# A 2-D Fourier transform and a gated feed-forward layer on one core: second weight chunk folded in halves around the second stage, weight bits of two chunks made later, fewer and larger spills

## The chip, the cores and the metric

The kernel runs on one core of a Trainium2 chip. The metric is the device time of one launch in microseconds (us); lower is better. The times shown are medians of several executions. One more execution was recorded by the hardware profiler, and every duration below comes from that recording. Engines are named as the profile names them: PE is the matmul engine and PEld its weight loads, DVE, ACT and POOL are the three elementwise engines, and SP issues the DMAs.

## The reference

x is (8, 3008, 256), w_in (256, 2048), w_out (2048, 256), all float32; the output is (24064, 256).

```python
X = np.fft.fft(x, axis=1)          # over the sequence, 3008 = 47 * 64
X = np.fft.fft(X, axis=2).real     # over the width, 256
h = X.reshape(24064, 256) @ w_in
g = h * (1.0 / (1.0 + np.exp(-1.702 * h)))
out = g @ w_out
```

## The kernel before

**The pieces of the computation.** The transform over the width is not done on the data. It is multiplied into the first weight matrix instead: `fold_w(n)` multiplies a cosine and a sine matrix by 512 columns of w_in (chunk n of four) and leaves the result in two tiles `wcs[0]` and `wcs[1]`; ACT copies it there out of two PSUM banks called `psw`. The transform over the sequence has two stages. The first one (`mix_first` for batch 0; `fold1` on POOL with `mix1` on PE for batches 1 to 7) leaves its result in the tile `xt`, or `made` for batch 0. `spill` writes it to device memory `Td`, `fill` reads it back in another order as the tile t4, `rotate` multiplies one column, and `stage2` does the second stage on PE; DVE transposes its result out of PSUM (L361) into `pq`.

**The steps.** Each of the 8 batches has 3 blocks of 512 rows, each block two halves of up to 256 rows, and each half goes through 8 steps, one for each pair of 128-column pieces of the 2048 hidden columns: 384 steps, 48 to a batch. A step is a first matmul (pq times wcs), the activation, and a second matmul (`product`) with `wo`, the second weight matrix. Steps 0 to 7, while the weights are still being made, use a plain form: `hidden(t)` (two PSUM banks pa and pb, L183; ACT copies pa to v, L519), `rows(t)` on DVE (L557, L560, L548: sums of pa, pb and the row nb that `nyquist` made), `activate(t)` on ACT, `product(t)`, issued three steps later. From step 8 on, both matmuls have a form with fewer multiplications and more sums on DVE and POOL (`begin`, `forward`, `backward`, `sums`, `small_products`). Chunk n of w_in serves steps 2n and 2n+1 of each half, and chunk n of w_out likewise.

**Weights.** Both matrices are converted chunk by chunk from 64-bit words of which the kernel uses the two 32-bit halves. For one chunk: `load_in`/`load_out` (a DMA of 1 MB into one of three `raw` slots), `squares` (ACT L405), `clamp` (POOL L410), `low_up` and `low_down` (ACT L415, L420), `high` (three DVE operations, L437 to L439, called the masks below; the last leaves the masked word in the ring "a"), and the adding of the low bits, `finish_in` (POOL L451, into the tile `wst`) or `finish_out` (two POOL operations L459, into `wo`). `bounds` is squares, clamp, low_up and low_down together. The call takes the chunk's key: in0 to in3 and out0 to out3. The tile `big` holds these buffers as rings: "s" (squares), "m" (clamped words), "r" (low bits), "a", "raw", "h" (the activations of the plain steps).

**What sets the order.** There is no scheduler: every engine carries out its own instructions in the order of the program text, and semaphores hold an instruction until its operands are there. The opening is written out by hand up to `finish_out(0)`. Then one loop runs over the steps; `at(t, fn)` puts a call at the end of step t, `early` puts `fold_w(2)` and `fold_w(3)` inside steps 3 and 5, and `rows_at` puts `first_row(n)` (small matmuls `psf` from row 0 of wcs[1], copied to af1 and af2 by ACT) inside steps 1, 4 and 6. All DMAs of the main loop stand in one queue on SP, also in the order of the text, and each waits for the landing of the one eight places before it. `paced(t)` is a DMA of one word out of the data that step t makes; as SP issues in order, it holds back the DMAs after it until then.

**Banks.** `spare` is a list of six PSUM banks, b0 b1 b2 o2 o3 o4. Each call of `bank` takes the first and puts it at the end, so who meets whom in a bank depends on the number of calls before. `hidden(5)` names its banks b0 and b1 outright. `warm(1)` is one matmul of 128x512 whose result nobody reads; it takes a bank too.

**Later batches.** In batch b (starting at step t0 = 48 b; `late` is 5 for batch 0 and 0 for the others), the next batch's first stage runs in steps t0+6 to t0+21 on POOL; each of the four `mix1` is followed a step later by two spills of 192 KB; `fill` is issued in three parts from t0+27, `rotate` at t0+36, and `stage2` of the next batch at t0+40. The x of the batch after that is loaded from t0+31.

Of the kernel before, what the change touches and what calls it, by code (L numbers as in the profile page):

```python
# [46 lines left out]
def view(ap, offset, *dims):  # L47
    return bass.AP(ap.tensor, ap.offset + offset, [list(d) for d in dims])
# [63 lines left out]
def kernel(ctx: ExitStack, tc, x, w_in, w_out, tab1, tab2, out):  # L112
# [17 lines left out]

    Xr = [nc.dram_tensor(f"Xr{b}", (NA, NJ, D), F32, kind="Internal").ap() for b in range(B)]
    Nd = nc.dram_tensor("Nd", (B * NBLK, 512), F32, kind="Internal").ap()
    Tk = nc.dram_tensor("Tk", (B * NBLK * NF, 1), F32, kind="Internal").ap()
    Td = [nc.dram_tensor(f"Td{b}", (NG * 128, D), F32, kind="Internal").ap() for b in range(B)]

    w1 = const.tile([128, (NJ + 3) * NM + 64 - NM], F32, tag="w1", name="w1")
# [13 lines left out]
    o_banks = [psp.tile([128, 512], F32, tag=f"o{i}", name=f"o{i}") for i in range(2)]  # L150
    rest = psu.enter_context(tc.tile_pool(name="psu", bufs=1, space=PS))
    big = cv.tile([128, 19 * 1024], F32, tag="big", name="big")
    rings = {"s": (0, 1024, 3), "a": (3072, 1024, 1), "raw": (4096, 2048, 3), "h": (10240, 1024, 4), "r": (14336, 1024, 2),
             "m": (16384, 1024, 2)}
    turns = {}

# [11 lines left out]
    def bank(name, tag=None):  # L168
        if tag is None:
            tag = spare.pop(0)  # L170
            spare.append(tag)
        if tag in ("o0", "o1"):
            return o_banks[int(tag[1])]
        return (rest if tag[0] == "o" else psp).tile([128, 512], F32, tag=tag, name=name)
# [149 lines left out]
        for _ in range(n):  # L324
            nc.tensor.matmul(ps[:], lhsT=wcs[0][:, 0:128], rhs=wcs[0][:, 0:512], start=True, stop=True)

    def spill(b, c, q):

        nc.sync.dma_start(out=view(Td[b], (16 * c + 4 * q) * D, [NJ * D, NM], [1, 4 * D]),
                          in_=xt[64 * c:64 * c + NM, 4 * q:4 * q + 4, :].rearrange("p q d -> p (q d)"))  # L330

    def fill(b, a0=0, a1=NG):
        if a0 == 0:
# [42 lines left out]
    def nyquist_out(b, blk):  # L376
        i = b * NBLK + blk
        nc.sync.dma_start(out=Nd[i:i + 1, :], in_=pqt[b, blk][0:1, 1, :])

    def paced(t):  # L380
        nc.sync.dma_start(out=Tk[t:t + 1, :], in_=big[0:1, at_left(t, A11):at_left(t, A11) + 1])

    raw = {}

# [83 lines left out]
        for out, i0, i1 in ((t1, b12, b11), (t2, b22, t1), (t3, b22, b12), (t4, b21, t2)):  # L468
            nc.gpsimd.tensor_tensor(out, i0, i1, op=ALU.subtract)

    def fold_w(n):
        ps = [bank("psw") for _ in range(2)]
        for i in range(2):
            for cs in range(2):
                halves(ps[cs][:], cd[:, i, cs, :], wst[n][:, i, :], start=(i == 0), stop=(i == 1))
        for cs in range(2):

            nc.scalar.copy(wcs[cs][:, n * 512:(n + 1) * 512].rearrange("p (f c) -> p f c", f=4),
                           free(ps[cs][:], 0, [1, 4], [4, 128]))
# [42 lines left out]
    def at_left(t, q):  # L522
        return LEFT + t % 4 * 1024 + q * 256
# [356 lines left out]
        spill_first(k, 16, NM, (nc.sync, nc.sync))  # L880
    prepare(in1)
    squares(in1, nc.scalar)
    for h0 in (0, 512):
        finish_in(0, h0, 512)
    clamp(in1)
    low_up(in1)
    low_down(in1)
    high(in1)
    load_out(1, nc.sync)
    fill(0, 4, NG)  # L890
    warm(1)
    fold_w(0)
    warm(1)
    first_row(0)
    prepare(out0)
    finish_in(1)
    clamp(out0)
    rotate(0, 0, 4, nc.scalar.copy)
    squares(out0, nc.scalar)
    stage2(0, 0)  # L900
    warm(1)
    low_up(out0)
    low_down(out0)
    high(out0)
    load_in(3, nc.sync)
    prepare(in2)
    squares(in2, nc.scalar)
    clamp(in2)
    fold_w(1)
    finish_out(0)  # L910

    extra, early = {}, {}

    def at(t, fn, *args):
        extra.setdefault(t, []).append((fn, args))

    n = len(steps)

    for t, key in (1, in2), (2, ("out", 1)), (3, ("in", 3)), (5, ("out", 2)), (6, ("out", 3)):
        at(t, high, key)  # L920
        if key != in2:
            at(t - 1, bounds, key)
        at(t + 1, finish, key)
    early[3], early[5] = 2, 3
    rows_at = {1: 1, 4: 2, 6: 3}
    for t, c in ((0, 2), (1, 3)):
        at(t, load_out, c, nc.sync)
    at(3, load_matrices)
    if B > 1:
# [8 lines left out]
    for b in range(B):  # L938
        t0 = b * NBLK * NF
        late = 0 if b else 5  # L940
        if b + 2 < B:
            for k in range(3):
                at(t0 + 11 + k, paced, t0 + 11 + k)
                at(t0 + 11 + k, turn, b + 2, k)
        if b + 1 < B:
            for c in range(NCH):
                for part in range(2):
                    at(t0 + 6 + 2 * c + part + late, fold1, b + 1, c, part, nc.gpsimd)
                if c % 2:
                    k = t0 + 9 + 2 * c + late + (late > 0 and c == 5)  # L950
                    at(k, mix1, b + 1, c // 2)
                    for half in range(2):
                        at(k + 1, spill, b + 1, half, c // 2)
            for blk in range(NBLK):
                at(t0 + 27 + blk + late, paced, t0 + 27 + blk + late)
                at(t0 + 27 + blk + late, fill, b + 1, 4 * blk, 4 * blk + 4)
            if b + 2 < B:
                for k in range(4):
                    at(t0 + 31 + 2 * k + late, paced, t0 + 31 + 2 * k + late)
                    at(t0 + 31 + 2 * k + late, load_x, b + 2, k)  # L960
            at(t0 + 36 + 3 * (late > 0), rotate, b + 1)
        for blk in range(NBLK):
            nxt = (b, blk + 1) if blk + 1 < NBLK else (b + 1, 0)
            if nxt[0] < B:
                at(t0 + blk * NF + 8, stage2, *nxt)
                at(t0 + blk * NF + 9, nyquist_out, *nxt)
                at(t0 + blk * NF + 10, nyquist, *nxt)

    for t in range(n + LAG):
        if t < NP:  # L970
            if t == NP - 3:
                spare[:] = [tag for tag in spare if tag[0] == "o"] + ["b2"]
            hidden(t)
            if t == NP - 1:
                middle(NP)
                begin(NP)
                for c0 in range(0, DF, 1024):
                    nc.sync.dma_start(out=wcs[1][0:1, c0:c0 + 1024], in_=tab1[127:128, n0 + 4:n0 + 1028])
            if t == 0:
                low_up(in2)  # L980
                nyquist(0, 0)
                low_down(in2)
            if t in rows_at:
                first_row(rows_at[t])
            if t >= LAG:
                product(t - LAG, 0, None)
            if t in early:
                fold_w(early[t])
            if t:
                activate(t - 1)  # L990
            rows(t)
            if t == NP - 1:
                doubled(NP)
                middle(NP + 1)
        else:
            after, special = (any(fn in (mix1, stage2) for fn, _ in extra.get(k, ())) for k in (t - 1, t))
            if t < n:
                begin(t, 1)
            if t == NP:
                activate(t - 1)  # L1000
            if t < n:
                forward(t)
            if after and t + 1 < n:
                middle(t + 1)
            opening = (t - LAG) % NP == 0 and t >= NP + LAG
            one, other = (t - LAG, (1, 2, 4, 7)), (t - LAG - 1, (5, 6, 3))
            if opening:
                small_products(*other)
            cut = 0 if opening and not after else 3 if after else 2
            product(t - LAG, 0, cut)  # L1010
            if after:
                small_products(one[0], one[1][:1])
                small_products(other[0], () if opening else other[1][:1])
            if t + 1 < n:
                begin(t + 1)
            if not opening:
                small_products(other[0], other[1][after:])
            product(t - LAG, cut, 6 if t - LAG == last else None)
            small_products(one[0], one[1][after:])
            swap(t - LAG - 2)  # L1020
            if t < n:
                backward(t)
            if t + 1 < n:
                doubled(t + 1)
            if t < n:
                activate_back(t)
                sums(t, nc.gpsimd)
            if t + 2 < n and not special:
                middle(t + 2)
            combine_small(t - LAG - 1)  # L1030
            if t - LAG == last:
                product(last, 6, None)
            sums(t - 1, nc.vector)
            deeper(t - 2, 0)
            deeper(t - 3, 1)
        if t == NP:
            psu.close()
            low = ctx.enter_context(tc.tile_pool(name="low", bufs=1, space=PS))
            pot["low"] = low.tile([128, 3 * 512], F32, tag="low", name="low")
        if t >= LAG:  # L1040
            combine(t - LAG)
            combine_last(t - LAG - 2)
            turn_last(t - LAG - 3, 0)
            turn_last(t - LAG - 4, 1)
        if t >= NP:
            spare[:] = [f"b{t % 2}"] * special + ["b2"]
        for fn, args in extra.get(t, ()):
            fn(*args)
# [28 lines left out]
```

## Time and profile before

| | us |
|---|---|
| median of 3 runs (1861.98 to 1864.17) | 1862.27 |
| the profiled execution's own time | 1861.98 |
| its span on the core | 1860.2 |
| mean granted PE clock, share of full | 0.999 |
| PE busy | 1843.6 (99% of the span) |
| DVE / ACT / POOL busy | 1522.8 / 1150.2 / 963.2 |
| first matmul of step 0, `hidden(0)` | 39.85 |
| first matmul of step 5, `hidden(5)` | 63.20 |
| start of step 48 to start of step 96 (batch 1 to batch 2) | 276.11 to 501.58 |

The opening, in which the weights are converted and the first batch is transformed, lies in the first 86 us; step 8, the first of the second form, follows it. From there the batches repeat every 225.1 to 225.5 us. In a row of a stretch by engines the columns are the stretch, its length, the busy time and count of instructions of PE, PEld, DVE, ACT, POOL and SP, the granted clock, the busy share of the DMA engines, and what they moved in GB/s. A row of a timeline gives the start, the duration, the engine, the line, the operation, out <- in, the shapes, how many instructions went together, and in square brackets the idle time before it and who ended it. A row of the waits names the waiting group, the one that released it, the idle us in sum, how many, and the longest.

### The profile page before, as it was taken

What the parts mean: (1) busy time and instruction counts of PE and PEld (TensorE: products, weight loads), DVE (VectorE), ACT (ScalarE), POOL (GpSimd) and SP (SyncE); (2) the same over time, 40 slices, a digit from 0 to 9 for tenths busy, and PEclk for the clock granted to TensorE, in tenths of its full rate; (3) what the DMA queues carried; (4) which work ended last, traced back from release to release, by engine and by line L of the source; (5) the groups of instructions that cost most, each with busy time, mean ns of one, the idle gap of its engine ahead of it and who ended that gap; (6) DMA issues with size and microseconds to landing.
All of it is one profiled execution on the core that took longest, in us unless ns stands there. A gap on an engine that the chain in (4) does not pass through costs nothing.

```text
span 1860.2 us, 56005 instructions
## 1 busy us (share of the span) xinstructions
PE 1843.6 (99%) x23684; PEld 1404.9 (76%) x23684; DVE 1522.8 (82%) x2229; ACT 1150.2 (62%) x2248; POOL 963.2 (52%) x1057
## 2 busy tenths in 40 slices
PE   8999999999999999999999999999999999999998
PEld 5677777777777777777777777777777777778776
DVE  7888788888798877987789878888888888878874
ACT  6656666666656656666665666656666666656663
POOL 4676446744367444773347643476445754434442
PEclk9999999999999999999999999999999999999999
DMA  8721340215012240213302132031411111100111
GB/s 269 190 61 34 80 72 19 71 49 102 19 35 56 67 84 18 60 37 87 63 13 65 44 86 52 17 76 34 102 30 25 36 46 35 31 19 13 22 20 24
DMA packets 148507, 105.31 MB, mean 57 GB/s; under 512 B 105961, under 2 KB 129033, under 8 KB 147744
## 3 DMA queue, kind: packets, MB, share of 16 engines
q1 hardware_dynamic: 147040, 101.20, 23.7%
q8 instruction: 187, 3.06, 0.7%
q10 hardware_dynamic: 1216, 0.52, 0.1%
q14 instruction: 64, 0.52, 0.1%
HBM read 64.41 MB, written 48.05 MB: 60 GB/s over the span
## 4 chain that ended last, share of the span: by engine, by line
PE 87%; DVE 6%; ACT 3%; POOL 1%; DMA 1%; issue 1%; SPq 0%; DVEq 0%; ACTq 0%; POOLq 0%
PE x L183 32%; PE o L183 24%; PE low L668 23%; PE o L668 4%; DVE big L634 2%; PE ps L355 1%; PE ps L254 1%; DVE big L769 1%; DVE big L548 1%; ACT x L575 1%; DMA big<-in_moe_w_in_dram 1%; ACT big L590 0%; DVE big L612 0%; DMA wo<-in_tab_dram 0%; ACT g L587 0%
## 5 line engine op out<-in xcount | busy, mean ns | idle before, releaser
L605 POOL TENSOR_TENSOR big<-big 128x256 f32<-128x256 f32 (+1 forms) x376 | 349.9, 931 | 840.0 <-ACT big L597 732.2
L183 PE MATMUL x<-pq,wcs 128*64 128x256 f32 (+1 forms) x6016 | 771.3, 377 | 3.5 <-ACT g L587 2.2
L634 DVE TENSOR_TENSOR big<-big 128x512 f32<-128x512 f32 (+1 forms) x736 | 636.2, 879 | 30.6 <-PE low L668 14.2
L183 PE MATMUL o<-big,wo 128*64 128x256 f32 (+1 forms) x4800 | 621.1, 375 | 0.0
L183 PEld LDWEIGHTS x<-pq,wcs 128*64 128x64 f32 x6016 | 410.0, 137 | 193.7 <-issue 15.0
L183 PEld LDWEIGHTS o<-big,wo 128*64 128x64 f32 x4800 | 341.8, 137 | 146.7 <-DVE big L612 0.5
L587 ACT ACTIVATE g<-x 128x512 f32<-128x512 f32 (+1 forms) x376 | 222.0, 590 | 372.8 <-PE x L183 371.7
L548 DVE TENSOR_TENSOR big<-g,x 128x512 f32<-128x512 f32 (+2 forms) x440 | 253.8, 588 | 200.2 <-ACT big L590 199.8
L668 PE MATMUL low<-big 128*64 128x128 f32 (+1 forms) x5888 | 381.8, 270 | 0.0
L575 ACT ACTIVATE x<-nb,af 128x256 f32<-128x256 f32 (+1 forms) x752 | 352.7, 469 | 12.2
L606 POOL TENSOR_TENSOR big<-big 128x256 f32<-128x256 f32 (+1 forms) x376 | 358.7, 954 | 0.0
L668 PEld LDWEIGHTS low<-big 128*64 128x64 f32 x5888 | 337.0, 137 | 28.7
L590 ACT ACTIVATE big<-x 128x512 f32<-128x512 f32 (+1 forms) x376 | 220.5, 587 | 195.4 <-PE x L183 161.5
L597 ACT ACTIVATE big<-big 128x512 f32<-128x512 f32 (+1 forms) x376 | 231.8, 617 | 42.3 <-DVE big L548 40.4
L668 PE MATMUL low<-big,wo 128*64 128x128 f32 (+1 forms) x2944 | 220.2, 270 | 0.1
L668 PEld LDWEIGHTS low<-big,wo 128*64 128x64 f32 x2944 | 171.9, 137 | 3.8 <-DVE big L634 0.4
L613 DVE TENSOR_TENSOR big<-big 128x512 f32<-128x512 f32 (+1 forms) x188 | 147.7, 786 | 6.5
L612 DVE TENSOR_TENSOR big<-big 128x512 f32<-128x512 f32 (+1 forms) x188 | 136.9, 728 | 5.4 <-POOL big L605 5.4
L769 DVE TENSOR_TENSOR big<-big,low 128x512 f32<-128x512 f32 (+3 forms) x184 | 109.1, 610 | 3.5
L668 PEld LDWEIGHTS o<-big,wo 128*64 128x64 f32 x1472 | 92.2, 137 | 25.0
L668 PE MATMUL o<-big,wo 128*64 128x128 f32 (+1 forms) x1472 | 110.0, 270 | 0.0
L226 POOL TENSOR_TENSOR xt<-xt 111x510 f32<-111x510 f32 x56 | 77.2, 1379 | 4.4
(102 smaller groups left out, 965.0 us busy)
## 6 DMA issues: line engine op xcount, KB each, us to landing
out_dram<-os SPq DMA_DIRECT2D x284, 64.0 KB
t<-Td SPq DMA_DIRECT2D x22, 512.0 KB
Td<-xt SPq DMA_DIRECT2D x56, 192.0 KB
xt<-in_x_dram SPq DMA_DIRECT2D x14, 512.0 KB
xt<-Xr SPq DMA_DIRECT2D x14, 512.0 KB
nb<-Nd SPq DMA_DIRECT2D x23, 256.0 KB
out_dram<-os SPq DMA_DIRECT2D x96, 56.0 KB
Xr<-in_x_dram SPq DMA_DIRECT2D x7, 752.0 KB
```

Of the source, the lines that this page charges most:

```text
L183: nc.tensor.matmul(out[c0:c0 + 64], lhsT=lhs[:, c0:c0 + 64], rhs=rhs, skip_group_check=True, **how)
L548: nc.vector.tensor_tensor(free(out, at + m - 1, [by, 2], [RUN, blocks], [-1, m]), *ins, op=op)
L575: nc.scalar.activation(x[:, i * 256:i * 256 + n], nbt[b, blk][:, hh * 256:hh * 256 + n], ACTF.Copy, scale=af1[:, f:f + 1])
L587: nc.scalar.activation(two(g[:], n), two(xb[t][:], n), ACTF.Copy, scale=2.0)
L590: nc.scalar.activation(front(t), two(xb[t][:], width(t)), ACTF.Gelu_apprx_sigmoid)
L597: nc.scalar.activation(back(t), back(t), ACTF.Gelu_apprx_sigmoid)
L605: eng.tensor_tensor(right(t, S1, n), left(t, A21, n), right(t, A22, n), op=ALU.add)
L606: eng.tensor_tensor(left(t, S3, n), left(t, A11, n), left(t, A21, n), op=ALU.subtract)
L612: eng.tensor_tensor(s2, s1, a11, op=ALU.subtract)
L613: eng.tensor_tensor(s4, a12, s2, op=ALU.subtract)
L634: nc.vector.tensor_tensor(out, i0, i1, op=how)
L668: nc.tensor.matmul(o, lhsT=lhs, rhs=rhs, start=first_in, stop=(p == NP - 2), skip_group_check=True)
```

## The change

Seven things change together.

1. The tokens (`paced`, 63 one-word DMAs) are gone.
2. The first stage's result is spilled in two DMAs of 768 KB per batch, at steps t0+24 and t0+25 (+ late), in place of eight of 192 KB. `fill` and the load of the next x are issued one step later than before.
3. In the opening, `fold_w(1)` is split: its first half, over the first 128 rows of the chunk, stands before `rotate` and `stage2(0, 0)`, its second half after them; `high(in1)` and `finish_in(1)` are done in halves for it, and `clamp(in1)` stands between the two halves of `finish_in(0)`.
4. Two of the three `warm(1)` are gone.
5. `first_row(0)` stands after `fold_w(1)`; `finish_out(0)` moves to the end of step 1; `low_up(out0)` and `low_down(out0)` move into steps 0 and 1.
6. squares, low_up and low_down of in2 move into step 1, `bounds(out1)` from the end of step 1 to the end of step 2; the loads of out2 and out3 go from the ends of steps 0 and 1 to those of steps 1 and 2, and `load_in(3)` into step 0.
7. Ring "s" has two slots in place of three, ring "a" two in place of one.

```diff
-    rings = {"s": (0, 1024, 3), "a": (3072, 1024, 1), "raw": ...
+    rings = {"s": (0, 1024, 2), "a": (2048, 1024, 2), "raw": ...
...
-    def spill(b, c, q):
-        nc.sync.dma_start(out=view(Td[b], (16 * c + 4 * q) * D, [NJ * D, NM], [1, 4 * D]),
-                          in_=xt[64 * c:64 * c + NM, 4 * q:4 * q + 4, :].rearrange("p q d -> p (q d)"))
+    def spill(b, c):
+        nc.sync.dma_start(out=view(Td[b], 16 * c * D, [NJ * D, NM], [1, 16 * D]),
+                          in_=xt[64 * c:64 * c + NM, 0:16, :].rearrange("p q d -> p (q d)"))
...
-    def paced(t):
-        nc.sync.dma_start(out=Tk[t:t + 1, :], in_=big[0:1, at_left(t, A11):at_left(t, A11) + 1])
...
-    def fold_w(n):
-        ps = [bank("psw") for _ in range(2)]
-        for i in range(2):
+    folded = {}
+    def fold_w(n, parts=(0, 1)):
+        if parts[0] == 0:
+            folded[n] = [bank("psw") for _ in range(2)]
+        ps = folded[n]
+        for i in parts:
             for cs in range(2):
                 halves(ps[cs][:], cd[:, i, cs, :], wst[n][:, i, :], start=(i == 0), stop=(i == 1))
+        if parts[-1] == 0:
+            return
...
-    for h0 in (0, 512):
-        finish_in(0, h0, 512)
+    finish_in(0, 0, 512)
     clamp(in1)
+    finish_in(0, 512, 512)
     low_up(in1)
     low_down(in1)
-    high(in1)
+    for h0 in (0, 512):
+        high(in1, h0, 512)
     load_out(1, nc.sync)
     fill(0, 4, NG)
     warm(1)
     fold_w(0)
-    warm(1)
+    prepare(out0)
+    for h0 in (0, 512):
+        finish_in(1, h0, 512)
+    clamp(out0)
+    fold_w(1, (0,))
+    rotate(0, 0, 4, nc.scalar.copy)
+    stage2(0, 0)
+    squares(out0, nc.scalar)
+    fold_w(1, (1,))
     first_row(0)
-    prepare(out0)
-    finish_in(1)
-    clamp(out0)
-    rotate(0, 0, 4, nc.scalar.copy)
-    squares(out0, nc.scalar)
-    stage2(0, 0)
-    warm(1)
-    low_up(out0)
-    low_down(out0)
     high(out0)
-    load_in(3, nc.sync)
     prepare(in2)
-    squares(in2, nc.scalar)
     clamp(in2)
-    fold_w(1)
-    finish_out(0)
...
-    for t, key in (1, in2), (2, ("out", 1)), (3, ("in", 3)), (5, ("out", 2)), (6, ("out", 3)):
+    at(1, finish_out, 0)
+    at(1, high, in2)
+    at(1, finish, in2)
+    at(2, bounds, ("out", 1))
+    for t, key in (2, ("out", 1)), (3, ("in", 3)), (5, ("out", 2)), (6, ("out", 3)):
         at(t, high, key)
-        if key != in2:
+        if t > 2:
             at(t - 1, bounds, key)
         at(t + 1, finish, key)
...
-    for t, c in ((0, 2), (1, 3)):
+    for t, c in ((1, 2), (2, 3)):
         at(t, load_out, c, nc.sync)
...
-                    for half in range(2):
-                        at(k + 1, spill, b + 1, half, c // 2)
+            for c in range(2):
+                at(t0 + 24 + c + late, spill, b + 1, c)
             for blk in range(NBLK):
-                at(t0 + 27 + blk + late, paced, t0 + 27 + blk + late)
-                at(t0 + 27 + blk + late, fill, b + 1, 4 * blk, 4 * blk + 4)
+                at(t0 + 28 + blk + late, fill, b + 1, 4 * blk, 4 * blk + 4)
...
             if t == 0:
-                low_up(in2)
                 nyquist(0, 0)
-                low_down(in2)
+                low_up(out0)
+                load_in(3, nc.sync)
+            if t == 1:
+                low_down(out0)
             if t in rows_at:
                 first_row(rows_at[t])
+            if t == 1:
+                squares(in2, nc.scalar)
+                low_up(in2)
+                low_down(in2)
```

Here `finish(in2)` stands at the end of step 1, right after `high(in2)`; before, it stood at the end of step 2, behind `bounds(out1)`, which stood at the end of step 1.

More of the change, by code (lines that the diff above doesn't have):

```diff
@@ L132 @@
     Nd = nc.dram_tensor("Nd", (B * NBLK, 512), F32, kind="Internal").ap()
-    Tk = nc.dram_tensor("Tk", (B * NBLK * NF, 1), F32, kind="Internal").ap()
     Td = [nc.dram_tensor(f"Td{b}", (NG * 128, D), F32, kind="Internal").ap() for b in range(B)]
@@ L152 @@
     big = cv.tile([128, 19 * 1024], F32, tag="big", name="big")
-    rings = {"s": (0, 1024, 3), "a": (3072, 1024, 1), "raw": (4096, 2048, 3), "h": (10240, 1024, 4), "r": (14336, 1024, 2),
+    rings = {"s": (0, 1024, 2), "a": (2048, 1024, 2), "raw": (4096, 2048, 3), "h": (10240, 1024, 4), "r": (14336, 1024, 2),
              "m": (16384, 1024, 2)}
@@ L942 @@
             for k in range(3):
-                at(t0 + 11 + k, paced, t0 + 11 + k)
                 at(t0 + 11 + k, turn, b + 2, k)
@@ L949 @@
                 if c % 2:
-                    k = t0 + 9 + 2 * c + late + (late > 0 and c == 5)
-                    at(k, mix1, b + 1, c // 2)
-                    for half in range(2):
-                        at(k + 1, spill, b + 1, half, c // 2)
+                    at(t0 + 9 + 2 * c + late + (late > 0 and c == 5), mix1, b + 1, c // 2)
+            for c in range(2):
+                at(t0 + 24 + c + late, spill, b + 1, c)
             for blk in range(NBLK):
-                at(t0 + 27 + blk + late, paced, t0 + 27 + blk + late)
-                at(t0 + 27 + blk + late, fill, b + 1, 4 * blk, 4 * blk + 4)
+                at(t0 + 28 + blk + late, fill, b + 1, 4 * blk, 4 * blk + 4)
             if b + 2 < B:
                 for k in range(4):
-                    at(t0 + 31 + 2 * k + late, paced, t0 + 31 + 2 * k + late)
-                    at(t0 + 31 + 2 * k + late, load_x, b + 2, k)
+                    at(t0 + 32 + 2 * k + late, load_x, b + 2, k)
             at(t0 + 36 + 3 * (late > 0), rotate, b + 1)
```

## The prediction

> **What bounds the kernel now.** I read the page's busy table first, then the busy time by stretch, then the waits of PE, then the timelines of the opening on all five queues.
>
> ```profile
> PE 1843.6 (99%) x23684; PEld 1404.9 (76%) x23684; DVE 1522.8 (82%) x2229; ACT 1150.2 (62%) x2248; POOL 963.2 (52%) x1057
> ```
> ```profile
> 20.00:40.00 20.00, 18.17 (x176) 10.35 (x176) 13.25 (x16) 14.21 (x21) 11.13 (x8) 1.00 0.74 277
> 40.00:64.00 24.00, 22.67 (x210) 13.70 (x206) 22.18 (x30) 20.74 (x29) 12.00 (x8) 1.00 0.99 329
> 64.00:86.00 22.00, 21.18 (x194) 13.48 (x192) 15.86 (x22) 12.48 (x21) 16.94 (x16) 1.00 0.81 125
> 276.00:501.00 225.00, 224.39 (x2952) 172.69 (x2950) 187.93 (x273) 140.50 (x278) 119.23 (x132) 1.00 0.24 53
> ```
> ```profile
> PE psw L183 <- POOL wst L451: 2.5, 4, 0.9
> PE pb L183 <- DVE big L548: 0.8, 1, 0.8
> PE psf L183 <- DVE big L548: 0.7, 1, 0.7
> ```
> ```profile
> 36.36 3.65 PE L183 MATMUL psw<-wst,small 128*64 128x512 f32 x16 [0.92 <-POOL wst L451]
> 39.85 1.03 PE L183 MATMUL pa<-pq,wcs 128*64 128x256 f32 x8
> 63.20 1.06 PE L183 MATMUL pa<-pq,wcs 128*64 128x256 f32 x8
> ```
> ```profile
> 25.88 1.37 DVE L438 TENSOR_SCALAR big<-big 128x512 uint32<-128x512 uint32 x1
> 52.33 1.61 DVE L437 SCALAR_TENSOR_TENSOR big<-big 128x1024 f32<-128x1024 f32 x1
> 54.05 1.49 DVE L438 TENSOR_SCALAR big<-big 128x1024 uint32<-128x1024 uint32 x1
> 55.57 1.23 DVE L439 SCALAR_TENSOR_TENSOR big<-big 128x1024 uint32<-128x1024 uint32 x1
> 64.01 0.69 DVE L548 TENSOR_TENSOR big<-pa,dif 128x512 f32<-128x512 f32 x1
> ```
> ```profile
> 25.40 1.57 POOL L451 TENSOR_TENSOR wst<-big 128x512 uint32<-128x512 uint32 x1 [1.89 <-ACT e L309]
> 41.69 2.51 POOL L459 TENSOR_TENSOR wo<-big 128x512 uint32<-128x512 uint32 x2 [2.00 <-DVE big L439]
> 45.29 1.25 POOL L410 TENSOR_SCALAR big<-big 128x1024 f32<-128x1024 f32 x1 [1.09 <-DMA big<-in_moe_w_out_dram]
> 50.48 2.38 POOL L451 TENSOR_TENSOR wst<-big 128x1024 uint32<-128x1024 uint32 x1 [3.94 <-DVE big L439]
> 52.83 2.15 POOL L410 TENSOR_SCALAR big<-big 128x1024 f32<-128x1024 f32 x1
> ```
>
> PE is the bound: in a later batch of 225 us it idles 0.6. From 20 to 86 us it idles 66 - 62.02 = 3.98 us, and that is all the opening could give back, with 2 x 0.86 for two dropped warm matmuls. In 40 to 64 DVE is busy 22.18 of 24 us, so there it is a bound of its own. It and POOL also hold each other up: L438 took 1.37 us (0.43 when alone) and ended 0.29 after POOL's add; L437 at 52.33 took 1.61 (1.23 alone), the clamp at 52.83 took 2.15 (1.15 alone), the L438 after it 1.49 (0.69 alone). I therefore count L437 to L439 and POOL's operations as taking turns.
>
> **The fold of the second chunk.** clamp(in1) (1.18) now follows the first half add on POOL, 26.97 to 28.15; DVE's last L439 of in0 (was 27.29) waits for it and ends at 28.8. The second half add shares with the first L437 of in1 and ends at 30.1 to 30.8 (was 29.40). in1's masks run in halves of 0.69 + 0.43 + 0.69, each L438 behind an add of 1.27: adds end near 33.3 to 33.8 and 35.7 to 36.1 (the whole add ended at 36.31). PE: half a fold (1.86) from 33.4 to 33.9, rotate and stage2 (1.3), the other half, and first_row (0.55, moved from 32.38): hidden(0) starts at 38.5 to 39.3, not 39.85. That is 0.6 to 1.35 us earlier. The two warm matmuls stood in waits for POOL (0.92 us idle still followed the second), so dropping them gives nothing of its own.
>
> [...] The row: PE's last matmul ends at 1854.3 and the granted clock stays 1.00 until 1858.3, so 4 us without work cost no clock, and my longest new gap is 1.9. [...]
>
> **DVE up to step 2.** stage2 now lies between the half folds, so its transposes end at 37.8 to 38.5 (were 35.87); out0's masks then end at 42.0 to 42.8 (were 41.52). rows(0) no longer waits for pb and nb (0.33 + 0.88), so rows(1) ends at 46.2 to 47.1 (was 47.12). But finish_out(0) (2.51 on POOL, was at 41.69 beside rows, which take their operands from PSUM) now waits for low_down(out0), which ACT does in step 1: it starts at 44.5 to 45.5 and falls on in2's L437. in2's masks end at 50.3 to 51.1 (were 50.31). What the fold won is spent here.
>
> **Bits of out1.** They move from step 1 to step 2. There finish(in2) stands ahead of them on POOL: add 2.36, then clamp(out1) 1.15, so L437 of out1 can start at 53.9 to 54.7 and not at 52.33. POOL's next instruction, clamp(in3), is queued (in3 landed at 51.97) and may take its turn first, another 1.05. The masks take 1.23 + 0.69 + 1.23: they end at 57.1 to 58.9, against 56.80. I take 58.3 (+1.5), with POOL first, because POOL's back-to-back clamps at 65.12 and 66.23 leave no gap, while DVE wakes on a semaphore. ACT's extra work there (out1's and in3's six operations in a row, 6.7 us from about 50.4) ends near 57, and v(3) with it: hidden behind the 58.3. With DVE on time it would cost about 1 us. rows(3), in3's masks and rows(4) take 7.9 us as before (56.80 to 64.70): rows(4) ends at 66.2.
>
> **A bank falls differently.** PSUM banks go round a list of six. Before hidden(0) the kernel drew 20 (warm 1, mix 8, warm 1, fold 2, warm 1, first_row 1, rotate 1, stage2 2, warm 1, fold 2); the change draws 18. hidden(5) names b0 and b1. Before, fold_w(2) held them last, so hidden(5) started at 63.20 while rows(4) ran until 64.70. Now hidden(4) holds them, and hidden(5) must wait for rows(4): 66.2 + 0.1 = 66.3. That is +3.1 us for PE (PE itself gets there at about 64.7, as hidden(4) waits for ACT's copies of fold_w(2); so the bank alone is 1.6 of it). Queued behind hidden(5) on PE are product(2), fold_w(3) and all later steps; ACT's v(5) and rows(5) wait for it. Later waits follow from PE itself (pb of step 7 waits 0.82 for rows(6), which wait for PE's pa), so nothing is won back.
>
> **DMA queue, ring buffers and later batches: 0.** SP loses 63 tokens of one word, and eight spills of 192 KB a batch become two of 768 KB. Spills have landed 2.5 to 2.7 us after issue, the second of a pair 0.5 later. Two of four times the size, issued at step 24 (389 us in the batch from 276.1, 4.69 us a step), land by about 396. The fills are issued at steps 28 to 30 (third one at 423.06 before, landed 427.3); rotate is due at step 36, 445 us. 17 us cover it; beyond that each us late is one on PE, in seven batches. Without tokens the x and reversed-x loads go out earlier, behind stores that run 8 steps ahead of their buffers' reuse. load_in(3) waits for low_up(out0), about 43.4 (42.24 before); the queue is full with out1 and fill until 49.4. load_out(3) waits for clamp(out1), 54 to 55 (48.60 before), so the queue may run dry for 2 us and the row for wcs lands at 86 (84.04 before); PE wants it at 84.73 + 3.1. The second mask buffer ("a") takes away a wait of in1's second half and costs nothing.
>
> **Sum.** The profiled execution took 1861.98 us (span 1860.2, 1.8 around it), the lowest of three; the median is 0.29 above. 1861.98 + 3.1 = 1865.1; on the median 1865.4, that is +0.17%. A bound of 0.2% (3.7 us) is about what a measurement of this kernel can tell from no change. The ends of out1's masks, 57.1 and 58.9, give +1.9 and +3.7.
>
> **Rivals.**
> (B) More is lost, +4 to +8: every handover between DVE and POOL that I counted as free (six in the half folds, at some 0.1) or once (a turn is 1.05 to 2.4) falls badly, or the dry queue reaches out2, out3 or the wcs row. For it: DVE has 1.8 us of slack in 24. Against: out2 landed at 54.46 and was first read after 60. About 1867.5.
> (C) DVE wins the turn against clamp(in3), or rows(4) end before PE asks: only ACT's late copies remain, +0.5 to +1.9, about 1863.6.
> (D) Not slower: the 0.6 to 1.35 us of the earlier hidden(0) pass through, 1861.2. It decides at one point, the end of clamp(out1): before 52.4 us it costs DVE nothing, for which in2's masks must end by 48.8, 1.5 earlier than they do now. Against it stands finish_out(0) on POOL at that very time.
> (E) The change does not do what it says, i.e. the fold ends no earlier because DVE's halves are held up by adds: 39.85 stays, and the rest of the sum holds; within B.
>
> **How the numbers follow.** Forecast 0.57 (its part above 1866.0: 0.24, since the small handovers all point up), B 0.26, C 0.12, D 0.05 (0.04 of it below 1858.5, as something unseen in 1780 us of later steps). Slower: 0.24 + 0.26 = 0.50; faster 0.04; same 0.46. Range: from C's 1863.0 to 1869.0 in B. The forecast's own range is 1863.9 to 1866.9.
>
> **What would show it.** Right: the first pa matmul at 38.5 to 39.3; POOL with two L406 clamps straight after the 2.4 us L447 add, near 52 to 54, and DVE idle 1.5 us before L433; a new PE wait for DVE L550 before pa, 1.5 us, near 66; batches still 225.1 apart; PE idle in 20 to 86 us up from 4.0 to about 9. Wrong: spills or fills among PE's waits, a granted clock below 1.00 near 35 us, or rows(4) ending before 65.

## The result and the profile after

The changed kernel takes 1869.68 us (median of 14 runs, 1866.01 to 1872.09), the kernel before 1862.51 us (14 runs): a ratio of 1.0037, 95% interval 1.0028 to 1.0045. The forecast was slower, 1865.4 us (1863.0 to 1869.0). The direction was right; the loss, 7.2 us, is more than twice the 3.1 that were forecast and lies 0.7 us outside the range.

The profiled execution of the changed kernel took 1868.89 us, its span is 1867.1. First the page's busy times, then the busy time by stretch (the three rows of the opening and a later batch):

```profile
PE 1842.7 (99%) x23680; PEld 1420.0 (76%) x23680; DVE 1525.4 (82%) x2232; ACT 1150.2 (62%) x2248; POOL 963.9 (52%) x1058
```
```profile
20.00:40.00 20.00, 17.13 (x182) 9.83 (x180) 16.48 (x20) 12.20 (x20) 12.51 (x9) 1.00 0.75 275
40.00:64.00 24.00, 20.42 (x184) 12.09 (x183) 21.89 (x28) 21.47 (x29) 11.29 (x8) 1.00 0.84 284
64.00:86.00 22.00, 19.76 (x180) 13.08 (x178) 13.70 (x22) 12.14 (x19) 14.03 (x14) 1.00 0.94 161
276.00:501.00 225.00, 223.67 (x2944) 177.37 (x2942) 186.46 (x272) 139.89 (x277) 118.84 (x132) 1.00 0.26 54
```

PE idles 66 - (17.13 + 20.42 + 19.76) = 8.69 us between 20 and 86 us, where it idled 3.98 before. The last row matters as much: PE idles 1.33 us in a later batch, against 0.61. The waits of PE name both places:

```profile
PE psw L182 <- POOL wst L447: 2.9, 3, 1.6
...
PE low L670 <- issue: 1.9, 1, 1.9
PE o L182 <- ACT big L568: 1.5, 1, 1.5
PE pa L182 <- ACT wcs L480: 1.5, 1, 1.5
PE pa L182 <- DVE t L341: 1.4, 1, 1.4
PE pb L182 <- DVE big L550: 0.8, 1, 0.8
PE o L182 <- issue: 0.7, 1, 0.7
```

Beside the waits for a chunk's words (`psw`), four are waits of the opening: product(0) for activate(0) (1.5), hidden(4) for ACT's copies of fold_w(2) (1.5), hidden(5) for DVE's last operations of step 4 (1.4) and the old one at step 7. The two with "issue" are new in kind: PE waited for nothing that the profile shows, and both lie in later batches.

Dividing the loss: step 8 starts 2.92 us later than before (88.71 against 85.79 us, first `forward` on ACT). From there the seven stretches from batch start to batch start took 190.32, 225.47 and five times about 225.12 us before, and 190.33, 226.42, 225.14, 225.14, 226.06, 227.28, 225.15 now. The excess of three batches, 0.95 + 0.94 + 2.16 = 4.05 us, with 2.92 makes 6.97, the difference of the spans (6.9). So the opening lost what was forecast, and the later batches, forecast at nothing, lost more. The 2.92 is one execution's figure: in the profiles of the six runs below that have the same new opening, step 8 starts 1.91 to 3.77 us later than before, and in `steady_only`, which has the old opening, 1.40 us later.

### The profile page after: what moved, and what is told of

Same layout as the page of the kernel before. It is cut to its first block, busy times and chain, and to the rows that moved or that the text cites. A ratio compares the mean times of both kernels' runs of the same rounds, so it can differ in the third digit from the quotient of the medians.

```text
span 1867.1 us, 55815 instructions
## 1 busy us (share of the span) xinstructions
PE 1842.7 (99%) x23680; PEld 1420.0 (76%) x23680; DVE 1525.4 (82%) x2232; ACT 1150.2 (62%) x2248; POOL 963.9 (52%) x1058
## 4 chain that ended last, share of the span: by engine, by line
PE 85%; DVE 6%; ACT 3%; DMA 2%; POOL 1%; issue 1%; SPq 1%; DVEq 0%; ACTq 0%; POOLq 0%
PE x L182 32%; PE o L182 24%; PE low L670 23%; PE o L670 4%; DVE big L636 2%; PE ps L354 1%; PE ps L253 1%; DVE big L771 1%; DVE big L550 1%; DMA wcs<-in_tab_dram 1%; ACT x L577 1%; DMA big<-in_moe_w_in_dram 1%; DMA Xr<-in_x_dram 1%; ACT big L592 0%; DVE big L614 0%
## 5 line engine op out<-in xcount | busy, mean ns | idle before, releaser
L182 PEld LDWEIGHTS x<-pq,wcs 128*64 128x64 f32 x6016 | 417.8, 137 | 188.0 <-issue 16.2
L182 PEld LDWEIGHTS o<-big,wo 128*64 128x64 f32 x4800 | 348.6, 137 | 142.9 <-POOL wo L455 1.9
L670 PEld LDWEIGHTS o<-big,wo 128*64 128x64 f32 x1472 | 93.4, 137 | 24.2 <-issue 0.3
## 6 DMA issues: line engine op xcount, KB each, us to landing
nb<-Nd SPq DMA_DIRECT2D x23, 256.0 KB
```

Of the source, the lines that this page charges most:

```text
L182: nc.tensor.matmul(out[c0:c0 + 64], lhsT=lhs[:, c0:c0 + 64], rhs=rhs, skip_group_check=True, **how)
L670: nc.tensor.matmul(o, lhsT=lhs, rhs=rhs, start=first_in, stop=(p == NP - 2), skip_group_check=True)
```

## The later batches: PE waits for its own code

The largest single loss, in the timeline of PE at 1303 us:

```profile
1303.13 0.61 PE L670 MATMUL low<-big 128*64 128x128 f32 x8
1303.57 0.27 PE L670 MATMUL low<-big,wo 128*64 128x128 f32 x1
1305.69 0.55 PE L670 MATMUL low<-big,wo 128*64 128x128 f32 x6 [1.85 <-issue]
```

PE stops inside a run of eight equal matmuls, after the first of them, and the profile names nobody who released it. The page's list of DMA queues has one for instructions:

```profile
q1 hardware_dynamic: 144226, 101.20, 25.0%
q8 instruction: 187, 3.06, 0.7%
```

Queue 8 moved 187 packets of 16,384 bytes. The trace has 23,684 matmuls, as many weight loads and 500 other instructions on PE (47,868 in the kernel before): 256.0 per packet, so these packets are taken for PE's code, 256 instructions to a block. For the n-th packet one can count how many instructions PE had started when it began, less 256 n. In the kernel before this number has a median of 179 and is at most 272; call it the lateness of a block. In the changed kernel PE's longest pause near each of the late blocks 36, 106, 110 and 129 (0.42 to 2.13 us from one start to the next) comes when it has started exactly 449 instructions beyond 256 n, as if it had run out of them. For the blocks next to the stops (lateness, and start in us, worked out from the trace):

```
block         36             106             129
before        175 ( 392.58)  215 (1068.80)   205 (1292.43)
changed       422 ( 402.40)  410 (1079.15)   445 (1303.38)
PE stops       +0.93          +0.36           +1.97
```

These three stops make 3.26 of the 4.05 us. A fourth block, 110, came at 367 (1118.94 us), behind the loads of x, and PE lost 0.57 us near it; in the profiles of seven runs it comes at 348 to 379 and 0.1 to 0.9 us are lost there, and with it on time (250, `with_tokens`) nothing. The other late blocks of the changed kernel behind the opening, at 292 to 377, cost 0.2 us or less each. What held block 129 up stands in the traffic of those microseconds: the two spills were issued at 1294.78 and 1295.14 us, their 96 packets of 16,384 bytes took 1.20 us each (mean; 96 packets of 4,096 bytes of two of the old spills took 0.24), the second landed at 1305.20, and block 129 began at 1303.38, when the burst had almost drained. Block 36 began at 402.40; the last of its burst's packets began at 401.40.

## The experiments

Each median is compared with that of the kernel before in the same job (1862.36 to 1862.76 us), and a difference such as +2.97 is against it. With some ten executions each, the 95% intervals reach about 1.7 us to either side, so two medians less than a microsecond apart are not told apart. Theory F: the later batches lose because the new DMA traffic holds up PE's code. Rival O: they lose nothing of their own, and all of the 7 us belongs to the opening. For the opening the theory is the prediction's, a bank and out1's late masks, against ACT's late copies and against DVE as the bound.

**The two halves of the change.** `steady_only` is the kernel before with items 1 and 2 of the change alone; `opening_only` is the changed kernel with those taken back.

> The kernel before with only the later-batch part of the change: no tokens, two spills of 768 KB, fill and x loads a step later; the opening as before. Theory F (PE's code blocks, 16 KB packets on the instruction queue, are held up behind the new DMA traffic, and PE runs dry): the opening costs nothing, single batches take 0.3 to 2.2 us more than 225.12, sum +3.6 to +4.3, about 1866.5, with a spread of some 4 us between executions. Rival O (all is in the opening, and other executions lose there what the profiled one lost later): 1862.5, every batch 225.1.

Measured: 1864.30 (11 runs, 1862.51 to 1869.17), ratio 1.0018 (1.0009 to 1.0027). The profiled execution (1866.95) has its opening's waits much as before (step 8 starts 1.40 us later, though) and the same three blocks late (36 at 432, 106 at 419, 129 at 449) in batches of 226.43, 225.75 and 227.28 us:

```profile
PE low L664 <- issue: 2.1, 1, 2.1
PE x L182 <- issue: 1.1, 1, 1.1
```

The median is +1.9 and not +3.6 to +4.3: six executions lie between 1862.5 and 1864.3, five between 1866.6 and 1869.2. The loss is there or not there, execution by execution.

> The changed kernel with tokens, eight spills, fill and x loads of before: only the opening is changed. Theory F: step 8 starts 2.9 to 3.6 us later than before, every batch 225.1, about 1865.7, spread as before (3 us). Rival O: 1869.7, all of the loss.

Measured: 1865.33 (1864.28 to 1867.55), ratio 1.0016 (1.0007 to 1.0025): +2.97, and behind the opening no block later than 273. Rival O falls; the opening costs what the forecast's sum said.

**Tokens, or the size of the spills?**

```diff
# small_packets: four spills of 192 KB where the change has one of 768 KB
-                at(t0 + 24 + c + late, spill, b + 1, c)
+                for q in range(4):
+                    at(t0 + 24 + c + late, spill, b + 1, c, q)
# eight_spills: each pair behind its mix1, as before; no tokens
+                    for half in range(2):
+                        at(k + 1, spill, b + 1, half, c // 2)
# with_tokens: the changed kernel, and before each turn, fill and load_x
+                    at(t0 + 32 + 2 * k + late, paced, t0 + 32 + 2 * k + late)
```

> The changed kernel, but each spill of 768 KB is issued as four of 192 KB in the same step: the same bytes at the same time, in packets of 4 KB where the profile of the changed kernel shows 96 of 16 KB at 1.2 us each. If the packet's size is what holds the code blocks up: at most a quarter of the later loss stays (that of the x loads), about 1866.5. If the burst of 1.5 MB in two steps is what counts, whatever its packets: 1869.7 as the change.

Measured: 1865.62 (1864.41 to 1871.18), +3.26. The same 1.5 MB in the same two steps, in 384 packets of 4,096 bytes from 390.97 to 399.80 us; block 36 began at 395.97, in the middle of them, with a lateness of 190. PE's waits after 95 us:

```profile
PE x L182 <- ACT g L589: 2.2, 6, 0.4
PE x L182 <- PE low L670: 0.7, 1, 0.7
PE x L182 <- ACT x L577: 0.4, 2, 0.2
```

No "issue" is left, and at the spills nothing is lost. The wait of 0.7 us stands at 1121 us, behind block 110, which came at 379 while the loads of x moved packets of 2,048 bytes. One of the eleven executions took 1871.18 us, and it has no trace. The burst takes about as long (8.8 us from its first to its last packet, against 8.6) and moves as much. But the edit makes two things smaller at once, the packets and the DMAs (192 KB in place of 768 KB). Which of the two frees the code blocks is not shown: large DMAs in small packets at the spills were not run. The loads of x, DMAs of up to 512 KB in packets of 2,048 bytes, did hold block 110 up (379), so the packet's size alone is not the whole answer.

> The changed kernel with eight spills of 192 KB behind their mix1 as before, but still without tokens, and fill and x loads as in the change. If the two large spills are the whole later loss: 1865.7. If the x loads, which without tokens go out in a bunch, share in it (late code blocks near 441, 667, 896 and 1119 us speak for that): 1866.5 to 1868. If it is all the tokens: 1869.7.

Measured: 1865.86 (1865.15 to 1867.92), +3.50. Without tokens the x loads still delay blocks (335 at 440, 377 at 895, 363 at 1117 us), and 0.5 us are lost at the last of these in the profiled execution. (In `opening_only`, with no block late there, the same batch is 0.5 us longer too, at other places.) By the medians the missing tokens are worth 0.3 to 0.6 us, which these medians cannot tell from nothing.

> The changed kernel with the tokens put back before turns, fills and x loads; the two spills of 768 KB stay. Theory F, spills: the late code blocks near 402, 1079 and 1303 us stay and cost 3 to 3.5 us in the profile, those near 441, 895 and 1118 us (x loads) go: 1869.2. If the missing tokens were the cause: 1865.3.

Measured: 1869.08 (5 runs, 1864.73 to 1871.71), +6.6. With tokens the blocks of the x loads (40 and 87, at 437.75 and 889.00 us) are at 260 and 191 again, and the three beside the spills stay at 422, 410 and 445. The tokens are not the cause.

**The burst's length and its phase.** `spills_apart` issues the second spill two steps after the first, `spills_later` both at t0+26.

> The changed kernel with its two spills of 768 KB two steps apart (t0+24 and t0+26) in place of one. In the changed kernel a pair keeps the DMA engines busy for about 10 us, and PE runs dry where its code block comes at instruction 410 or later of the 256 before it (160 to 200 is usual; 338 to 348 cost nothing). If it is the length of the burst: no block later than about 350 at the spills, what is left is the opening and at most 0.5 us for the x loads, 1865.8. If packets of 16 KB hold the code up whatever the burst: blocks past 400 stay, 1868 or more.

Measured: 1867.08 (1864.86 to 1868.37), +4.3. In the profiled execution (1865.89) the three blocks come at 325, 305 and 349 and PE does not stop at them; the median, between the two expectations, keeps 1.35 us over `opening_only`. Spreading the burst takes away most of the loss, not all.

> The changed kernel with its two spills both at t0+26, so that the same burst (two of 768 KB, 16 KB packets, some 10 us) starts about 7 us later in the batch. If PE loses because one of its code blocks falls due inside the burst, the loss follows the phase: in the profile of opening_only the blocks fall due, on the time of the changed kernel, at 395.7, 1071.9 and 1295.7 us (the ones that were late) and next at 403.8, 1079.4 and 1301.4. The later burst (about 400 to 409, 1076 to 1086, 1302.5 to 1312) holds blocks up by 5 to 7 us and none of these three batches loses 0.9 us or more, unless the block of 1301 falls just inside; 1865.7 to 1867.5. If the burst costs PE time by itself (memory, or another engine): batches 1, 4 and 5 lose what they lost before, 1869.5.

Measured: 1867.54 (10 runs, 1864.63 to 1868.93), +5.1, just above what was expected. The profiled execution follows the phase: blocks 36, 106 and 129 are on time (204, 211, 192), the burst delays others (37 at 356, 60 at 379), and the batches take 225.1 to 225.5 us. But it is the fastest of the ten; the others lose up to 4.3 us more, and they have no trace. That a block of code must fall due inside the burst fits the profiled executions; what differs in the others is open.

**The opening.** All are `opening_only` with one edit or more.

```diff
# opening_banks: hidden(0) to hidden(5) meet the banks of the kernel before
+    for _ in range(2):
+        spare.append(spare.pop(0))
# opening_in3: ACT's operations of in3 behind the copies of fold_w(2)
-            at(t - 1, bounds, key)          # bounds(in3) at the end of step 2
+            at(2, prepare, key); at(2, clamp, key)
+            at(3, squares, key, nc.scalar); at(3, low_up, key); at(3, low_down, key)
# opening_bits
-    at(2, bounds, ("out", 1))
+    at(1, bounds, ("out", 1))               # ahead of finish(in2)
```

> opening_only with the list of banks turned by two before step 0, so that hidden(0) to hidden(5) meet the banks of the kernel before. My prediction put 1.6 of its 3.1 us on the bank: then 1863.8, and no wait of hidden(5) for rows(4). In the profile of opening_only hidden(5) came at 66.97, after rows(4) (64.6), and the 2.9 us before hidden(4) were a wait for ACT's copies of fold_w(2). If those copies decide: 1865.3, unchanged.

Measured: 1864.98, +2.46, 0.5 less than `opening_only`, which the intervals cannot tell from no gain; 1.5 were expected if the bank decided. The wait at hidden(5) is gone from its profile; those at product(0) (1.5) and hidden(4) (1.3) stay.

> opening_only with squares, low_up and low_down of in3 (ACT, 3.4 us) moved behind ACT's copies of fold_w(2); the clamp stays. If those copies, queued behind in3's three operations, are the loss of the opening: the wait before hidden(4) falls from 2.9 us (1.5 in the changed kernel) to about 0.3, no dip of the clock follows, 1863.3 or less. If the banks and DVE (rows(4) at 65.4 to 66) bound it: PE waits at hidden(5) instead, 1865.

Measured: 1865.51, +2.99. hidden(4) waits no more, and the loss moves on to the next wait, for rows(3):

```profile
PE psf L183 <- DVE big L554: 2.1, 1, 2.1
PE o L183 <- ACT big L572: 1.5, 1, 1.5
PE pa L183 <- DVE t L342: 1.4, 1, 1.4
```

> opening_only with the bits of out1 back at the end of step 1, before finish(in2). My prediction's chain (finish(in2) and clamp(in3) on POOL ahead of DVE's first mask operation of out1, +1.5 us at rows(4)): DVE's L437 of out1 starts at 51.0 in place of 52.3, rows(4) ends 1.5 to 2 us earlier, ACT's six operations lie 2 us earlier too, 1863.3. If only ACT's wait for in3 (landed at 53.3) counts: 1865.3.

Measured: 1865.85, +3.33: nothing gained. L437 of out1 started at 54.86 us, later than in `opening_only` (52.30) where 51.0 was expected, since v(2) now stands behind out1's three operations on ACT and rows(2) waited 1.6 us for it. The edit was meant to help DVE; the engine that decided was ACT.

```diff
# opening_two: the banks, and of out1's bits only squares and clamp at step 1
+    at(1, squares, ("out", 1), nc.scalar); at(1, clamp, ("out", 1))
-    at(2, bounds, ("out", 1))
+    at(2, low_up, ("out", 1)); at(2, low_down, ("out", 1))
# opening_four: opening_two, opening_in3, low_up(out0) ahead of nyquist(0, 0), and
             if t == 1:
                 squares(in2, nc.scalar)
-                low_up(in2)
-                low_down(in2)
             if t:
                 activate(t - 1)
+            if t == 1:
+                low_up(in2)
+                low_down(in2)
```

> opening_only with two edits at once: the list of banks turned by two, and of out1's bits only squares and clamp back at the end of step 1 (low_up and low_down stay in step 2, so that v(2) on ACT is not held up as in opening_bits, where rows(2) waited 1.6 us for it). If the loss of the opening is two waits of like size that stand in for each other (the bank at hidden(5), 1.4 us, and out1's masks 2 us late on DVE with ACT's late copies beside them): no wait at hidden(5), rows(4) ends 2 us earlier, 1862.6, the time of the kernel before. If something else of the new opening costs the 3 us: 1865.

Measured: 1864.02 (1863.54 to 1865.75), +1.26. More than half of the opening's loss is gone, not all: product(0) still waits 1.5 us.

> opening_two, and also activate(0) ahead of in2's low_up and low_down, low_up(out0) ahead of nyquist's copy, and in3's operations behind ACT's copies of fold_w(2): every wait that the profile of opening_only shows is taken away. If DVE, which worked without a pause from 41 to 64.7 us in the kernel before, bounds the opening: no more than 0.2 us better than opening_two, 1862.4, and not under the kernel before by more than 0.5, although step 0 starts 1 us earlier. If PE bounds it: 1 to 1.5 us under the kernel before, 1861.2.

Measured: 1863.07 (1861.66 to 1864.29), +0.31, ratio 1.0003 (0.9995 to 1.0012). That is 0.95 us better than `opening_two`, where 0.2 at most was expected if DVE bounds the opening, and it misses the 1861.2 of a bound by PE. With the waits at product(0), hidden(4) and hidden(5) gone the new opening is as fast as the old one and no faster, although hidden(0) starts 12.95 us after the last `ps` matmul ended where it was 14.10 before. PE gives most of the difference back in one place (and 0.53 us at 85.31, where it waits for the DMA that loads row 0 of wcs[1], the "row for wcs" of the prediction):

```profile
46.87 3.65 PE L183 MATMUL o<-big,wo 128*64 128x256 f32 x32
52.79 3.65 PE L183 MATMUL psw<-wst,small 128*64 128x512 f32 x16 [2.27 <-POOL wst L451]
```

PE waits for in2's words, which wait for in2's masks; and DVE paused only once, for 0.43 us, between 41 and 64.4:

```profile
59.17 1.23 DVE L437 SCALAR_TENSOR_TENSOR big<-big 128x1024 f32<-128x1024 f32 x1 [0.43 <-ACT big L405]
```

So in this profile DVE sets the pace up to step 5 (hidden(5) at 63.03, before 63.20), and an earlier step 0 has nobody to use it. Its L437 took 2.00 us at 45.28 and 1.60 at 52.22, against 1.23 at 59.17; that POOL's operations beside it are the reason, as in the kernel before (1.61 beside a clamp of POOL, 1.23 alone), is an inference. That DVE alone is the bound was not tested by an edit that shortens its work. None of the variants beats the kernel before.

> The kernel before with one edit: the list of banks turned by four before step 0, so that hidden(4) and not fold_w(2) holds the banks that hidden(5) names. The price of the bank by itself: hidden(5) waits for rows(4) (63.20 to 64.8), +1.4 to +1.7, 1864.1. If PE wins it back in later waits (0.82 us at pb of step 7): under +0.8.

Measured: 1864.27 (1863.40 to 1868.51), +1.51. The bank by itself, on the kernel before:

```profile
PE pa L183 <- DVE t L342: 1.5, 1, 1.5
```

**Do the two losses add?** `four_and_spills` is `opening_four` with the change's spills and without tokens.

> opening_four with the later-batch part of the change (two spills of 768 KB at t0+24 and 25, no tokens): does the loss of the later batches add to that of the opening? In its profile the blocks of 402, 1079 and 1303 us should be late again. If the parts add as the change and opening_only say (7.2 - 3.0 = 4.2): 0.3 + 4.2 over the kernel before, 1867.0. If as steady_only says (1.9): 1864.8.

Measured: 1868.54 (9 runs, 1864.50 to 1872.20), +6.1, more than either sum. Blocks 36, 106 and 129 are late in its profile as in the change (423, 411, 446), and its batches exceed 225.12 by 1.3, 1.0 and 2.2 us. So three measurements of the spills' part give 1.9 (`steady_only`), 4.2 (+7.2 of the change less the +2.97 of `opening_only`) and 5.8 us (this one less `opening_four`), each with executions 6 us and more apart. The last holds something else as well. In its profile PE ran at half clock (0.50) from 53.6 to 57.0 us, after a wait of 2.23 us in the opening, so that fold_w(2) took 5.25 us in place of the 3.65 above; step 8 starts 1.3 us later than in `opening_four`:

```profile
53.77 5.25 PE L182 MATMUL psw<-wst,small 128*64 128x512 f32 x16 [2.23 <-POOL wst L447]
```

Six of its nine executions have a mean clock of 0.998 or less, and three of the eleven of `opening_four`. The sign of the spills' part is settled, and in the profiles its place; its size is some 2 to 4 us, or up to 6 with what the clock adds, and not better known.

## Why the prediction was right and wrong

Right, by its own steps:

- **The opening's sum.** +3.1 forecast, +2.97 measured (`opening_only`), +2.92 in the profile of the changed kernel. That it fits so well is partly luck: at hidden(5), where the sum was reckoned, the profile shows +2.46 (65.66 for 63.20), another 0.43 us were lost at 87.63 us, where PE waits for the DMA of the wcs row, and the path had another term (below).
- **The order on POOL.** Two clamps straight behind the 2.4 us add, and DVE idle until its first mask operation of out1 (1.74 us; 1.5 were forecast). POOL and DVE in the changed kernel:

```profile
49.82 2.38 POOL L447 TENSOR_TENSOR wst<-big 128x1024 uint32<-128x1024 uint32 x1 [1.98 <-DVE big L435]
52.17 2.44 POOL L406 TENSOR_SCALAR big<-big 128x1024 f32<-128x1024 f32 x2
```
```profile
53.50 2.20 DVE L433 SCALAR_TENSOR_TENSOR big<-big 128x1024 f32<-128x1024 f32 x1 [1.74 <-POOL big L406]
```

- **The bank.** hidden(5) waits for DVE's work of step 4, 1.43 us (1.5 forecast), at 65.66 (66.3 forecast); as an edit of its own it costs the kernel before 1.51. Taken back in the new opening it gave only 0.5, not the 1.6 of the sum, as other waits of the same size stood beside it. PE idle between 20 and 86 us: 8.69 (about 9 forecast).
- **What the fold won is spent.** hidden(0) came 1.76 us earlier (38.09, a little ahead of the forecast 38.5 to 39.3), 0.7 of it because the first stage had ended 0.7 us earlier in this execution, and product(0) starts at 48.63 us in both kernels.

Wrong:

- **"DMA queue, ring buffers and later batches: 0".** This is the step that failed. The spills' cover was reckoned against their readers (fills, rotate: 17 us), and those were indeed never late. What the longer burst held up was PE's code, another user of the DMA engines that the step did not list, though its queue stood in the page (q8, 187 packets). The working also took the old landing time and only scaled it: some 7 us from the first issue to the last landing, where 10.4 were measured (1294.78 to 1305.20). The loss is 3.26 us at three blocks of code in the profiled execution, and 4.05 with block 110 behind the loads of x, which the step let go out earlier at no price, and small remainders. Of the signs that the prediction named for this step, "batches still 225.1 apart" failed; "spills or fills among PE's waits", meant to show such a loss, did not appear, because the wait has no name but "issue". Rival B's 1867.5 is nearer to the time, but of its causes the profile shows only the late wcs row, 0.43 us.
- **The term for product(0) is missing.** Moving squares, low_up and low_down of in2 into step 1 put 3.3 us of ACT's work ahead of activate(0), which product(0) waits for: 1.50 us. ACT's late copies before hidden(4) were named but hidden behind DVE; PE waited 1.50 us for them. The sum came out right because the chain on DVE had been reckoned too long: out1's masks ended at 57.6, not 58.3, and rows(4) at 65.4, not 66.2.
- **"4 us without work cost no clock".** That was read after the kernel's last matmul, where no later work could show the price, and the row behind the one that was read has the lower clock (0.58 in the mean, from 1858.3 on at half):

```profile
1858.00:1860.00 2.00, 0.00 (x0) 0.00 (x0) 0.00 (x0) 0.00 (x0) 0.00 (x0) 0.58 0.36 76
```

So the clock fell some 4 us after the last matmul; that a pause of 4 us is free does not follow. In the profiled execution of `opening_only`, after ACT had waited for in3's DMA, PE stood still for 2.89 us and then ran at half clock for 7 us; product(1) took 5.39 us in place of 3.67:

```profile
57.69 1.38 PE L183 MATMUL pa<-pq,wcs 128*64 128x256 f32 x8 [2.89 <-ACT wcs L484]
...
61.66 5.39 PE L183 MATMUL o<-big,wo 128*64 128x256 f32 x32
```
```profile
56.00:58.00 2.00, 0.31 (x4) 0.24 (x6) 1.17 (x3) 2.00 (x4) 1.50 (x2) 1.00 1.12 298
58.00:60.00 2.00, 2.00 (x14) 1.23 (x12) 1.97 (x4) 1.67 (x3) 1.00 (x1) 0.59 0.91 192
60.00:62.00 2.00, 2.00 (x22) 1.23 (x20) 1.93 (x3) 0.23 (x3) 0.00 (x0) 0.50 1.05 368
62.00:64.00 2.00, 2.00 (x12) 1.10 (x10) 1.97 (x5) 2.00 (x4) 1.32 (x1) 0.50 1.06 384
```

A shorter pause, of 2.23 us in `four_and_spills`, was followed by half clock as well; one of 2.27 in `opening_four` was not (clock 1.00 from 40 to 64 us). What decides is not shown. In the profile of the changed kernel the clock stays 1.00. Of the 14 executions of the change four have a mean clock of 0.998, all of them between 1870.22 and 1872.09 us, and ten one of 0.999 or 1.000, 1866.01 to 1871.31 us; a part of the scatter may be this, but without their traces that is an inference.

## What to carry to other kernels

That its readers never wait does not make a transfer free: here two spills of 768 KB delayed PE's code, which came over the DMA engines too (187 packets of 16,384 bytes), and PE lost 3.26 us by it in the profiled execution. So look at the instruction queue in the DMA part of the page before making few large transfers out of many small ones, and where PE has no slack (busy 99% here) try the many small ones first (192 KB in packets of 4 KB lost nothing at the spills here). When a stage holds several waits of like size, taking one away shows little (0.5 us or nothing here); take them away together before saying what bounds it. A count of PSUM banks in a rotating list is part of an edit: dropping two dummy matmuls moved the banks, and moving them alone cost the kernel before 1.5 us.

## What the runs showed that was not expected

The two spills of 768 KB, in packets of 16,384 bytes, held PE's code blocks up until their burst had almost drained (lateness 445 of a usual 179), some 7 us: they began at 402.40, 1079.15 and 1303.38 us and were due at about 395.7, 1071.9 and 1295.7. The same bytes as eight DMAs in packets of 4,096 bytes did not (190 to 257). What the profile counts as a packet is one row of the spill (16 x 256 words of 4 bytes, 16,384 bytes); for how many of these packets a code block has to wait, and why, the runs do not show. Spread evenly over 16 DMA engines, 96 packets of 1.20 us are 7.2 us for each (an estimate from these numbers), about the measured delay, as if a block waited for all of one engine's share. But the small spills are 24 packets of 0.30 us, 7.2 us as well, and delayed nothing. Whether it is the size of a DMA or of its packets that decides, and why the wait grows to the length of the burst, is open.
